# Filler products in the planned idle gaps of TensorE, in an attention and gated-MLP kernel on one core

## The chip, the core and the metric

The kernel runs on one NeuronCore of a Trainium2 chip. Its engines work side by side, each on its own queue in order: TensorE (PE, matrix products into the accumulation memory PSUM), VectorE (DVE), ScalarE (ACT), GpSimd (POOL) and SyncE (SP), which issues the transfers (DMA). The metric is the device time of one execution in microseconds (us); the median of three runs is given, and less is better.

## The reference

Four batches of 8 heads with 768 positions and 64 features go through attention with a causal window of 128 and 4 sink positions, and the result through a gated MLP whose gate mixes positions:

```python
scores = np.where(keep, scale * q @ k.T, -1e9)   # keep: 4 sinks, or 0 <= rel < 128
a = softmax(scores); x = a @ v                   # heads side by side: (4, 768, 512)
h = relu(x @ w_in)                               # 512 -> 1024
u, v = h[..., :512], h[..., 512:]
v_n = (v - mean(v)) / sqrt(var(v) + 1e-6)
v_s = einsum('ts,bsd->btd', w_spatial, v_n) + b_spatial[None, :, None]
out = (u * v_s) @ w_out
```

## The kernel before

The work is cut into tiles of 128 positions, 6 to a batch. For each tile and each half of the heads there is one score product (`sc`, four banks of PSUM), masks and row maxima on DVE (`mask`, line 808), exponentials on ACT, a split of the weights into a high and a low 16-bit part on DVE, ACT or POOL (lines 557 to 573), their transposition by DMA (`pT`), the product with the values (`av`, lines 864 to 876, many small products of 65 columns) and the division by the row sums on DVE (`divide`, lines 878 to 884: `den` and then `x`). After each tile follow the MLP's products `ps_v` and `ps_u`, and per batch `ps_s` and `ps_o`; operands are split in two 16-bit parts, so each product is a sum of three (`three`, line 588). Batch 0's tiles also share the engines with the decoding and splitting of the weights (`w_in`, `w_spatial`, `w_out`), whose scales come from a maximum over all partitions (`all_max`, lines 600 to 624: a row transpose `ps_row` and a column product `ps_col` on PE with reductions on DVE between).

The order of everything is fixed when the kernel is built. Each piece is handed to a `Plan` with a rank (its step plus the entry of its kind in the table `WHEN`), the engines that may run it and an estimated time; `Plan.order` (line 293) then simulates the engines piece by piece with these times, taking the piece that can start earliest, and the pieces are recorded in order of their simulated starts. Each engine runs its part of that order strictly in turn. A ring of buffers is a number of slots; a piece that needs a new buffer has to wait in the plan until one is free.

The `av` ring has two slots, taken from a pool of PSUM banks, one tile to a bank:

```python
BANKS = {"sc": 4, "av": 2, "mm": 2}
IN_TURN = ("u", "vn", "q", "pexp", "pT", "p16", "xT", "x16", "av", "sc", "vraw")
"sc": ("sc", bank("sc")), "av": ("av", bank("av")),
```

The framework puts in the semaphore waits that the recorded order needs: for a tile's readers on its writers, and for a buffer's next writer on its last readers.

Of the kernel before, what the change touches and what calls it, by code (L numbers as in the profile page):

```python
# [6 lines left out]
F32 = mybir.dt.float32  # L7
F32R = mybir.dt.float32r
F16 = mybir.dt.float16
# [10 lines left out]
P = 128  # L20
# [244 lines left out]
GAP = {"o": 0.201, "s": 0.751, "u": 1.654, "v sum": 1.920, "w_in 0": 0.416, "w_in 1": 0.266, "w_out": 1.377, "w_sp": 0.683}  # L265
TOGETHER = 4
IN_TURN = ("u", "vn", "q", "pexp", "pT", "p16", "xT", "x16", "av", "sc", "vraw")
LATENCY = {"PE": 0.25, "d": 0.15, "a": 0.18, "p": 0.12}


# [7 lines left out]


QUEUED = 3.0  # L280


class Plan:

    def __init__(self, rings, ring_of):
        self.pieces, self.rings, self.ring_of = [], rings, ring_of

    def add(self, name, step, b, engines, time, f, reads=(), writes=(), dma=None, shared=False):

# [3 lines left out]
    def order(self):  # L293
# [21 lines left out]
        for i in range(n):  # L315
            for key in ps[i][5] + ps[i][6]:
                base = key[:2]
                ring = self.ring_of.get(base[0])
# [3 lines left out]
        held = {r: [] for r in self.rings}  # L322
        slots = {r: [None] * n for r, n in self.rings.items()}
# [4 lines left out]
        ready = [0.0] * n  # L328
        free = {"PE": 0.0, "d": 0.0, "a": 0.0, "p": 0.0, "SP": 0.0, "port": 0.0}
        moved = 0.0  # L330
        open_ = [i for i in range(n) if not missing[i]]
        out = []

        def room(i):

            t, new = 0.0, {}
            for key in ps[i][5] + ps[i][6]:
                base = key[:2]
                ring = takes.get(base)
                if ring is None or base in taken:  # L340
                    continue
                k = len(held[ring]) + new.get(ring, 0)
                if ring in IN_TURN and turn[ring][k] != base:
                    return None
                j = new[ring] = new.get(ring, 0) + 1
                if ring == "p16":
                    old = slots[ring][k % len(slots[ring])]
                    if old and left[old]:
                        return None
                    t = max(t, until[old] if old else 0.0)  # L350
                    continue
                ends = sorted(until[b] if b else 0.0 for b in slots[ring] if b is None or not left[b])
                if len(ends) < j:
                    return None
                t = max(t, ends[j - 1])
            return t

        while open_:
            best = None
            for i in open_:  # L360
                t = room(i)
                if t is None:
                    continue
                t = max(t, ready[i])
                if ps[i][7] and not ps[i][5]:
                    t = max(t, moved - QUEUED)
                es = ps[i][2] if ps[i][2] not in free else (ps[i][2],)
                cs = []
                for e in es:
                    port = e == "p" or (e == "d" and ps[i][8])  # L370
                    b = max(t, free[e])
                    d = ps[i][3][e] if isinstance(ps[i][3], dict) else ps[i][3]
                    cs.append((max(b, free["port"] if port else 0.0) + d, b, e))
                for c in ((min(cs),) if len(cs) > 1 else cs):
                    c = (c[1], i, c[2])
                    if best is None or c < best:
                        best = c
            if best is None:
                raise RuntimeError("plan: no piece can go on: " + str([(ps[i][0], ps[i][5], ps[i][6]) for i in open_[:16]])
                                   + str({r: [(b, b and left[b]) for b in h] for r, h in slots.items()}))  # L380
            t, i, e = best
            _, _, _, time, f, reads, writes, dma, shared = ps[i]
            d = time[e] if isinstance(time, dict) else time
            if e == "p" or (e == "d" and shared):
                d += max(free["port"] - t, 0.0)
                free["port"] = t + d
            free[e] = t + d
            if dma is None:
                end = t + d + LATENCY[e]
            else:  # L390
                moved = max(t + d + 0.3, moved) + dma
                end = moved + 1.5
            for key in reads + writes:
                base = key[:2]
                ring = takes.get(base)
                if ring and base not in taken:
                    taken.add(base)
                    held[ring].append(base)
                    k = ((len(held[ring]) - 1) % len(slots[ring]) if ring == "p16" else
                         min((until[b] if b else 0.0, k) for k, b in enumerate(slots[ring]) if b is None or not left[b])[1])  # L400
                    for j in users[base]:
                        ready[j] = max(ready[j], until[slots[ring][k]] if slots[ring][k] else 0.0)
                    slots[ring][k] = base
            for base in {k[:2] for k in reads + writes}:
                left[base] -= 1
                until[base] = max(until[base], end)
            open_.remove(i)
            for j in after[i]:
                missing[j] -= 1
                ready[j] = max(ready[j], end)  # L410
                if not missing[j]:
                    open_.append(j)
            out.append((t, len(out), f, e))
        if len(out) != n:
            raise RuntimeError("plan: pieces left")
        self.end = max(until.values())
        return [(f, e) for _, _, f, e in sorted(out, key=lambda x: x[:2])]


# [50 lines left out]
def fast_path(tc, st, qk, v, vs, w_in, w_sp, b_sp, w_out, out):  # L470

    nc = tc.nc
    TC = 256
    VNS = 2.0 ** 10
    with (
# [21 lines left out]
        def sb(shape, dt, tag):  # L497
            return lambda name: work.tile(shape, dt, tag=tag, name=name, bufs=RINGS[tag])

        def bank(tag):  # L500
            return lambda name: ps_all.tile([P, 512], F32, tag=tag, name=name, bufs=BANKS[tag])

        turns = {"p16": 0}

        def next_p16(name):
            turns["p16"] += 1
# [16 lines left out]
            "xT": ("xT", sb([P, 2, KC, TC], F16, "xT")),  # L523
            "g": ("g", sb([P, TC], F32, "g")),
            "g2": ("g2", sb([P, 2, TC], F32R, "g2")),
            "sc": ("sc", bank("sc")), "av": ("av", bank("av")),
            "ps_v": ("mm", bank("mm")), "ps_u": ("mm", bank("mm")), "ps_s": ("mm", bank("mm")),
            "ps_o": ("mm", bank("mm")), "ps_row": ("mm", bank("mm")), "ps_col": ("mm", bank("mm")),
        }
        rings = dict(RINGS, ksink=1, **BANKS)  # L530
        rings.update({f"{kind}{j}": 1 for kind in ("kslot", "vslot", "vsink") for j in range(4)})
        plan = Plan(rings, dict({k: r for k, (r, _) in makers.items()}, **{r: r for r in rings}))
        tiles = {}

        def tl(kind, i):
# [562 lines left out]
```

## Time and profile before

| | us |
|---|---|
| median of 3 runs | 440.31 (439.42 to 442.29) |
| profiled execution | 440.37 |
| its span, first to last instruction | 438.5 |
| TensorE busy in it | 400.7 |
| VectorE busy | 330.2 |
| ScalarE busy | 252.8 |
| GpSimd busy | 129.7 |

The profile is one execution. Busy time is the time in which an engine executes an instruction; weight loads of TensorE (PEld) overlap its products and are counted apart. [...] In the rows in order of time, equal instructions that follow each other are merged, with their count; the bracket at the end is idle time just before, and what ended it. A product's time contains its draining, which overlaps the next product, so the pace is read from the starts.

### The profile page before, as it was taken

How to read it: one execution, taken by the hardware profiler on the slowest of the kernel's cores; microseconds unless marked ns; L12 is line 12 of the kernel's file. 1: busy time of each engine (PE TensorE's matmuls, PEld its weight loads, DVE VectorE, ACT ScalarE, POOL GpSimd, SP SyncE). 2: the span in 40 equal slices, each digit the busy share in tenths (PEclk: the TensorE clock that was granted, in tenths of full speed). 3: DMA queues.
4: the chain of work that ended last, by engine and by line, in shares of the span. 5: the costliest groups of instructions: out<-in, count | busy, mean ns of one | idle time of the engine just before them, and what ended most of it. 6: DMA issues, size and time to landing. Idle time of an engine off the chain costs nothing.

```text
span 438.5 us, 9688 instructions
## 1 busy us (share of the span) xinstructions
PE 400.7 (91%) x3509; PEld 301.9 (69%) x3509; DVE 330.2 (75%) x1048; ACT 252.8 (58%) x561; POOL 129.7 (30%) x192
## 2 busy tenths in 40 slices
PE   1537897899899999999999999999999999999995
PEld 1324454675687777677777768868867788878883
DVE  2899999899988999999898998887470752426350
ACT  3989876897974776688778878843232111010101
POOL 4545623635652314134443166600020200000000
PEclk9999988999999999999999999999999999999998
DMA  6999999899894399999999877946204000010102
GB/s 211 280 350 289 223 212 244 189 226 172 199 241 87 78 211 199 227 200 181 212 220 213 165 177 129 157 90 150 50 25 111 11 1 33 16 72 25 49 24 80
DMA packets 149640, 66.14 MB, mean 151 GB/s; under 512 B 124880, under 2 KB 137936, under 8 KB 149584
## 3 DMA queue, kind: packets, MB, share of 16 engines
q1 hardware_dynamic: 149440, 65.44, 66.3%
q8 instruction: 29, 0.48, 0.5%
q14 instruction: 27, 0.22, 0.2%
q10 hardware_dynamic: 144, 0.00, 0.0%
HBM read 28.72 MB, written 6.29 MB: 80 GB/s over the span
## 4 chain that ended last, share of the span: by engine, by line
PE 75%; DVE 13%; DMA 5%; ACT 2%; issue 2%; SPq 1%; ACTq 0%; DVEq 0%
PE ps_s L591 22%; PE ps_o L591 16%; PE ps_u L591 12%; PE ps_v L591 11%; PE sc L803 8%; DVE pexp L808 3%; PE av L873 2%; PE av L874 2%; PE av L875 2%; DMA q<-qk_t 1%; DMA dec<-w_in 1%; DMA vraw<-v_s 1%; DMA dec<-w_out 1%; DVE p L573 1%; DVE vring L580 1%
## 5 line engine op out<-in xcount | busy, mean ns | idle before, releaser
L591 PE MATMUL ps_s<-wsp,vn 128*128 128x256 f16 x864 | 99.3, 273 | 0.0
L591 PEld LDWEIGHTS <-vn 128*128 128x128 f16 x864 | 83.5, 98 | 12.1 <-issue 2.4
L813 ACT ACTIVATE pexp<-pexp,nm 128x260 f32<-128x260 f32 (+1 forms) x192 | 82.7, 484 | 11.1 <-DVE nm L808 10.5
L803 PE MATMUL sc<-kring,q 64*128 64x260 f32 (+1 forms) x384 | 65.6, 427 | 13.8 <-DMA q<-qk_t 9.2
L591 PE MATMUL ps_u<-xT,win 128*128 128x256 f16 x576 | 69.6, 273 | 2.7 <-ACT vr L916 1.8
L591 PE MATMUL ps_o<-wout,g 128*128 128x512 f32 x288 | 71.0, 400 | 0.0
L591 PE MATMUL ps_v<-win,xT 128*128 128x512 f16 x288 | 68.4, 391 | 0.8 <-DVE allmax_r L619 0.5
L591 PEld LDWEIGHTS <-win 128*128 128x128 f16 x576 | 54.4, 98 | 13.9 <-issue 7.4
L591 PEld LDWEIGHTS ps_o<-wout,g 128*128 128x128 f32 x288 | 53.0, 188 | 13.3 <-issue 0.7
L803 PEld LDWEIGHTS sc<-kring,q 64*128 64x128 f32 x384 | 39.8, 204 | 28.5 <-DVE nm L808 9.2
L573 POOL TENSOR_TENSOR p<-pexp,p 128x16 f16<-128x16 f32 (+2 forms) x43 | 41.9, 981 | 43.7 <-ACT p L557 36.4
L977 DVE SCALAR_TENSOR_TENSOR g<-ps_s,isc,b_bc 128x256 f32<-128x256 f32 x48 | 23.2, 483 | 41.2 <-PE ps_s L591 40.9
L1004 ACT COPY ob<-ps_o 128x512 f32<-128x512 f32 x24 | 14.0, 585 | 66.9 <-PE ps_o L591 66.0
L591 PEld LDWEIGHTS <-xT 128*128 128x128 f16 x288 | 28.2, 100 | 34.2 <-issue 6.3
L956 ACT ACTIVATE u<-ps_u,icu 128x256 f32<-128x256 f32 x48 | 22.7, 472 | 40.4 <-PE ps_u L591 39.8
L873 PE MATMUL av<-vring,pT 128*128 128x65 f16 x352 | 38.7, 197 | 0.9 <-ACT vring L559 0.9
L874 PE MATMUL av<-vring,pT 128*128 128x65 f16 x352 | 38.4, 197 | 0.6 <-DVE vring L580 0.6
L875 PE MATMUL av<-vring,pT 128*128 128x65 f16 x352 | 38.4, 197 | 0.0
L557 ACT CAST p<-pexp 128x32 f16<-128x32 f32 (+2 forms) x65 | 37.6, 599 | 0.8 <-DMA pT<-p 0.5
L573 DVE TENSOR_TENSOR p<-pexp,p 128x1024 f16<-128x1024 f32 (+2 forms) x37 | 36.3, 989 | 0.3 <-ACT p L557 0.3
L873 PEld LDWEIGHTS <-pT 128*128 128x128 f16 x352 | 33.4, 100 | 3.2 <-issue 2.4
L874 PEld LDWEIGHTS <-pT 128*128 128x128 f16 x352 | 33.3, 100 | 1.8 <-issue 0.8
(120 smaller groups left out, 581.6 us busy)
## 6 DMA issues: line engine op xcount, KB each, us to landing
kring<-qk_t SPq DMA_DIRECT2D x24, 256.0 KB, 4.1
q<-qk_t SPq DMA_DIRECT2D x24, 256.0 KB, 4.1
vraw<-v_s SPq DMA_DIRECT2D x24, 256.0 KB, 3.8
out<-ob SPq DMA_DIRECT2D x24, 256.0 KB, 2.0
dec<-w_in SPq DMA_DIRECT2D x8, 512.0 KB, 7.1
wsp<-w_sp_t SPq DMA_DIRECT2D x6, 384.0 KB, 6.5
dec<-w_out SPq DMA_DIRECT2D x4, 512.0 KB, 4.7
pT<-p SPq DMA_TRANSPOSE x96, 3.5
```

The costliest lines, as they stand in the source:

```text
L557: nc.scalar.copy(o, x)
L573: eng[e].tensor_tensor(out=o, in0=x, in1=hi, op=ALU.subtract)
L591: nc.tensor.matmul(o, a, m, start=(i == 0), stop=(i == n - 1))
L803: nc.tensor.matmul(view(h + q)[0], tl("q", (b, t))[rows, hp, :], keys, start=True, stop=True)
L808: nc.vector.tensor_tensor_reduce(out=po, in0=o, in1=mask, scale=-0.125, scalar=3.0e38, op0=ALU.add, op1=ALU.min, accum_out=nm()[:, q:q + 1])
L813: nc.scalar.activation(po, po, AF.Exp, bias=nm()[:, q:q + 1], scale=-1.0)
L873: nc.tensor.matmul(o[:, h], ph, vh, start=(t < 2 and j == 0), stop=False)
L874: nc.tensor.matmul(o[:, h], ph, vl, start=False, stop=False)
L875: nc.tensor.matmul(o[:, h], pl, vh, start=False, stop=(j == nb - 1 and (t < 2 or h == HH - 1)))
L956: plan.add("u relu", r, b, "a", 0.365, lambda e: nc.scalar.activation(tl("u", (b, c0))[:, d, :], tl("ps_u", i)[:, :TC], AF.Relu, scale=val ...
L977: nc.vector.scalar_tensor_tensor(out=g(), in0=tl("ps_s", i)[:, :TC], scalar=vals["s", "sp"][1], in1=b_bc[:, t0:t0 + TC], op0=ALU.mult, op1 ...
L1004: plan.add("o copy", r, b, "a", 0.485, lambda e: nc.scalar.copy(tl("ob", i), tl("ps_o", i)), [("ps_o", i)], [("ob", i)])
```

## The change

After the plan is made, its order is kept, and every idle gap that the plan's own simulation shows on TensorE from 4 us on is looked up. Into each goes a number of filler products that by 0.108 us each would take half of the gap. A filler loads a 16-bit view of the identity matrix as weights and streams 248 columns of the same matrix into columns 264 to 511 of the first value bank; the value products use columns 0 to 259, so nothing reads the fillers' result. To have a fixed place for them, the two value banks become one tile `avs` with two halves that are used alternately (`next_av`), and `STRICT` makes the plan alternate too.

```diff
--- before.py
+++ after.py
@@ -265,6 +265,7 @@
 GAP = {"o": 0.201, "s": 0.751, "u": 1.654, "v sum": 1.920, "w_in 0": 0.416, "w_in 1": 0.266, "w_out": 1.377, "w_sp": 0.683}
 TOGETHER = 4
 IN_TURN = ("u", "vn", "q", "pexp", "pT", "p16", "xT", "x16", "av", "sc", "vraw")
+STRICT = ("p16", "av")
 LATENCY = {"PE": 0.25, "d": 0.15, "a": 0.18, "p": 0.12}
 
 
@@ -278,12 +279,13 @@
 
 
 QUEUED = 3.0
+WARM_FROM, WARM_SHARE, WARM_ONE = 4.0, 0.5, 0.108
 
 
 class Plan:
 
-    def __init__(self, rings, ring_of):
-        self.pieces, self.rings, self.ring_of = [], rings, ring_of
+    def __init__(self, rings, ring_of, warm):
+        self.pieces, self.rings, self.ring_of, self.warm = [], rings, ring_of, warm
 
     def add(self, name, step, b, engines, time, f, reads=(), writes=(), dma=None, shared=False):
 
@@ -328,6 +330,7 @@
         ready = [0.0] * n
         free = {"PE": 0.0, "d": 0.0, "a": 0.0, "p": 0.0, "SP": 0.0, "port": 0.0}
         moved = 0.0
+        busy = [(0.0, WARM_FROM)]
         open_ = [i for i in range(n) if not missing[i]]
         out = []
 
@@ -343,7 +346,7 @@
                 if ring in IN_TURN and turn[ring][k] != base:
                     return None
                 j = new[ring] = new.get(ring, 0) + 1
-                if ring == "p16":
+                if ring in STRICT:
                     old = slots[ring][k % len(slots[ring])]
                     if old and left[old]:
                         return None
@@ -385,6 +388,8 @@
                 d += max(free["port"] - t, 0.0)
                 free["port"] = t + d
             free[e] = t + d
+            if e == "PE":
+                busy.append((t, t + d))
             if dma is None:
                 end = t + d + LATENCY[e]
             else:
@@ -396,7 +401,7 @@
                 if ring and base not in taken:
                     taken.add(base)
                     held[ring].append(base)
-                    k = ((len(held[ring]) - 1) % len(slots[ring]) if ring == "p16" else
+                    k = ((len(held[ring]) - 1) % len(slots[ring]) if ring in STRICT else
                          min((until[b] if b else 0.0, k) for k, b in enumerate(slots[ring]) if b is None or not left[b])[1])
                     for j in users[base]:
                         ready[j] = max(ready[j], until[slots[ring][k]] if slots[ring][k] else 0.0)
@@ -414,6 +419,10 @@
         if len(out) != n:
             raise RuntimeError("plan: pieces left")
         self.end = max(until.values())
+        for (_, t), (t1, _) in zip(busy, busy[1:]):
+            count = int((t1 - t) * WARM_SHARE / WARM_ONE)
+            if count:
+                out.append((t + 0.05, len(out), self.warm(count), "PE"))
         return [(f, e) for _, _, f, e in sorted(out, key=lambda x: x[:2])]
 
 
@@ -500,7 +509,20 @@
         def bank(tag):
             return lambda name: ps_all.tile([P, 512], F32, tag=tag, name=name, bufs=BANKS[tag])
 
-        turns = {"p16": 0}
+        avs = ps_all.tile([P, 2, 512], F32, tag="avs", name="avs", bufs=1)
+        turns = {"p16": 0, "av": 0}
+
+        def next_av(name):
+            turns["av"] += 1
+            return avs[:, (turns["av"] - 1) % 2]
+
+        def warm(count):
+            lead, follow = st.ident.bitcast(F16)[:, :P], st.ident.bitcast(F16)[:, :248]
+
+            def f(e):
+                for _ in range(count):
+                    nc.tensor.matmul(avs[:, 0, 264:], lead, follow, start=True, stop=True)
+            return f
 
         def next_p16(name):
             turns["p16"] += 1
@@ -523,13 +545,13 @@
             "xT": ("xT", sb([P, 2, KC, TC], F16, "xT")),
             "g": ("g", sb([P, TC], F32, "g")),
             "g2": ("g2", sb([P, 2, TC], F32R, "g2")),
-            "sc": ("sc", bank("sc")), "av": ("av", bank("av")),
+            "sc": ("sc", bank("sc")), "av": ("av", next_av),
             "ps_v": ("mm", bank("mm")), "ps_u": ("mm", bank("mm")), "ps_s": ("mm", bank("mm")),
             "ps_o": ("mm", bank("mm")), "ps_row": ("mm", bank("mm")), "ps_col": ("mm", bank("mm")),
         }
         rings = dict(RINGS, ksink=1, **BANKS)
         rings.update({f"{kind}{j}": 1 for kind in ("kslot", "vslot", "vsink") for j in range(4)})
-        plan = Plan(rings, dict({k: r for k, (r, _) in makers.items()}, **{r: r for r in rings}))
+        plan = Plan(rings, dict({k: r for k, (r, _) in makers.items()}, **{r: r for r in rings}), warm)
         tiles = {}
 
         def tl(kind, i):
```

The plan itself comes out as before: with the fillers left out, every engine has the same instructions in the same order, and the general path behind the branch at the end isn't run. 210 fillers are added, each a weight load and a product. Their groups, in order: 5, 6, 5, 9, 13, 3, 19, 20, 6, 9, 22, 6, 2, 10, 9, 12, 9, 5, 1, 17, 4, 2, 1, 3, 1, 5, all before 100 us of the plan, and 6 near its end.

In the built program the waits are set by tile. Six divides (their first instruction, `den`) wait for a count of PE's semaphore that is reached only with the last filler of the group recorded ahead of them: behind the first two value products (22 fillers), the third (10), the fourth (12), the fifth (9), the sixth (1) and the fourteenth (5). Five fillers wait for a divide. Where a divide is recorded ahead of the next value product, that product now waits for it, though it writes the other half.

On TensorE at the beginning (`sc` is the score product of one tile and half of the heads; a count at the end merges equal rows), before:

```order
L803 MATMUL sc<-kring,q 128x128 x8
L803 MATMUL sc<-kring,q 128x260 x8
L608 MATMUL ps_row<-ident,allmax_m 1x128
L615 MATMUL ps_col<-allmax_304,ones 128x1
L608 MATMUL ps_row<-ident,allmax_m 1x128
```

and now:

```order
L524 LDWEIGHTS ident
L524 MATMUL avs<-ident 128x248
L825 MATMUL sc<-kring,q 128x128 x4
L524 LDWEIGHTS ident
L524 MATMUL avs<-ident 128x248
```

The first two score products stood next to each other; now 5 fillers stand ahead of the first and 6 between the two.

On TensorE behind the first two value products (`av`, then `avs`; the last row before is the next score product), before:

```order
L873 LDWEIGHTS pT
L873 MATMUL av<-vring,pT 128x65
L874 LDWEIGHTS pT
L874 MATMUL av<-vring,pT 128x65
L875 LDWEIGHTS pT
L875 MATMUL av<-vring,pT 128x65
L803 MATMUL sc<-kring,q 128x260 x4
```

and now:

```order
L896 LDWEIGHTS pT
L896 MATMUL avs<-vring,pT 128x65
L897 LDWEIGHTS pT
L897 MATMUL avs<-vring,pT 128x65
L524 LDWEIGHTS ident
L524 MATMUL avs<-ident 128x248
```

22 fillers stand between the last of the value products and the score product.

On VectorE, around the divides of these two products, now (names in brackets are the semaphores that an instruction waits for):

```order
L766 SCALAR_TENSOR_TENSOR vsink_137<-vsraw,v_scale,vsink_137 32x4x64 [waits DMAHW4_49]
L673 SCALAR_TENSOR_TENSOR w_467<-dec,w_467 128x512 [waits DMAHW2_49,DVE_49]
L903 TENSOR_SCALAR den<-avs 128x4 [waits PE_49]
L904 RECIPROCAL den<-den 128x4 [waits DVE_49]
L905 TENSOR_TENSOR x<-avs,den 128x256 [waits DVE_49]
L903 TENSOR_SCALAR den<-avs 128x4
```

Nothing moved here. The first `den` waits for the last of the 22 fillers, where it waited for the last of its own products; the second, which had a wait of its own, needs none behind it.

## Rows read from the trace of the kernel before

**Rows 1.** The page's first part: TensorE's busy us, share, instructions.

```profile
PE 400.7 (91%) x3509; PEld 301.9 (69%) x3509; DVE 330.2 (75%) x1048; ACT 252.8 (58%) x561; POOL 129.7 (30%) x192
```

**Rows 2.** Busy time by stretch: busy us by engine, granted clock, DMA share.

```profile
core 0: us, PE busy (x) PEld busy (x) DVE busy (x) ACT busy (x) POOL busy (x), PEclk, DMA share, GB/s
9.00:20.00 11.00, 7.62 (x33) 5.25 (x33) 10.01 (x44) 9.51 (x23) 3.94 (x5) 1.00 1.11 321
20.00:30.00 10.00, 2.36 (x9) 1.87 (x10) 8.75 (x25) 8.03 (x19) 5.19 (x3) 1.00 1.05 301
30.00:41.00 11.00, 7.98 (x38) 4.33 (x36) 10.77 (x35) 11.00 (x24) 5.90 (x7) 1.00 1.11 326
41.00:48.00 7.00, 6.70 (x40) 3.62 (x41) 6.62 (x20) 4.49 (x13) 6.01 (x6) 1.00 0.94 181
53.00:59.00 6.00, 5.55 (x41) 3.99 (x41) 5.25 (x21) 5.55 (x16) 3.29 (x3) 0.72 1.05 258
120.00:430.00 310.00, 310.00 (x2790) 242.14 (x2787) 224.30 (x699) 155.69 (x345) 72.31 (x101) 1.00 0.56 120
```

**Rows 3.** Waits of VectorE, first 125 us: total us, times, longest.

```profile
DVE den L881 <- PE av L875: 2.2, 3, 0.8
```

**Rows 4.** Order of time, TensorE: start, length, engine, line, work, idle before.

```profile
34.92 0.25 PE L874 MATMUL av<-vring,pT 128*128 128x65 f16 x1
34.98 0.24 PE L875 MATMUL av<-vring,pT 128*128 128x65 f16 x1
51.22 0.19 PE L874 MATMUL av<-vring,pT 128*128 128x65 f16 x1
51.25 0.20 PE L875 MATMUL av<-vring,pT 128*128 128x65 f16 x1
96.61 1.47 PE L591 MATMUL ps_u<-xT,win 128*128 128x256 f16 x12
```

**Rows 5.** Order of time: first two value products, and their divide.

```profile
33.79 0.22 PE L874 MATMUL av<-vring,pT 128*128 128x65 f16 x1 [0.64 <-DVE vring L580]
34.89 0.15 DVE L881 TENSOR_SCALAR den<-av 128x4 f32<-128x4 f32 x1
```

**Rows 6.** Order of time: third value product and divide.

```profile
41.30 0.37 PE L608 MATMUL ps_row<-ident,allmax_m 128*1 128x128 f32 x1 [0.72 <-DVE allmax_m L605]
42.92 0.58 PE L615 MATMUL ps_col<-allmax,ones 1*128 1x1 f32 x2
43.15 0.14 DVE L881 TENSOR_SCALAR den<-av 128x4 f32<-128x4 f32 x1
```

**Rows 7.** Order of time: around the fourth and fifth value product.

```profile
51.76 0.15 DVE L881 TENSOR_SCALAR den<-av 128x4 f32<-128x4 f32 x1
52.50 0.42 DVE L808 CUSTOM_DVE_ANT_0 pexp<-sc,m_odd 128x260 f32<-128x260 f32 x1
52.84 0.42 DVE L808 CUSTOM_DVE_ANT_0 pexp<-sc,m_odd 128x260 f32<-128x260 f32 x1
52.98 2.28 PE L803 MATMUL sc<-kring,q 64*128 64x260 f32 x8 [1.54 <-DVE nm L808]
56.95 0.16 DVE L881 TENSOR_SCALAR den<-av 128x4 f32<-128x4 f32 x1 [0.68 <-PE av L875]
```

**Rows 8.** Order of time, TensorE and VectorE, the start.

```profile
8.99 2.70 PE L803 MATMUL sc<-kring,q 64*128 64x128 f32 x16 [8.99 <-DMA q<-qk_t]
11.37 0.28 DVE L808 CUSTOM_DVE_ANT_0 pexp<-sc,m_first 128x128 f32<-128x128 f32 x1
29.28 0.69 DVE L641 TENSOR_SCALAR_CACHE_REDUCE w<-w 128x512 f32<-128x512 f32 x1 [0.74 <-ACT w L645]
```

**Rows 9.** Order of time: TensorE's last wait; a product behind a divide.

```profile
111.07 1.47 PE L591 MATMUL ps_u<-xT,win 128*128 128x256 f16 x12 [1.81 <-ACT vr L916]
190.12 0.43 DVE L883 TENSOR_TENSOR x<-av,den 128x256 f32<-128x256 f32 x1
190.46 0.19 PE L873 MATMUL av<-vring,pT 128*128 128x65 f16 x1
```

## The prediction

> **What bounds the kernel now.** I read the page's totals first, then busy time by stretch, then the waits, then the order of time around the places that change. TensorE (PE) is busy 400.7 us, 91% of the span [rows 1], so it looks like the bound everywhere. By stretch it is not [rows 2]. From 120 to 430 us PE is busy all 310.00 us: that part is PE's. Before it PE has room (2.36 of 10 us from 20 to 30) and VectorE (DVE) has none: 10.01 of 11, 8.75 of 10, 10.77 of 11 and 6.62 of 7 us in the four stretches from 9 to 48. PE's last wait of any size is the 1.81 us before 111.07 [rows 9], for an activation that stands behind DVE's work. So the end is the moment at which PE resumes there, plus some 327 us of PE work without a gap. A change before 111 us counts only by what it does to DVE's chain; a PE instruction added after 111 us counts in full.
>
> PE also runs slowly early. The granted clock is printed as 1.00 before 47 us, but the records tell otherwise: at 34.92 and 34.98 us products of 65 columns start 55 ns apart, at 51.22 and 51.25 us 30 ns [rows 4]. [...] Later the clock falls again: 0.72 over 53 to 59 us [rows 2], which includes scores (2.28 us) that follow 1.54 us of idling [rows 7]. All this slowness has cost DVE little: up to 125 us it waited for a value product 2.2 us, three times [rows 3].
>
> **The change, part by part.** 210 fillers (each a weight load and a product of 248 columns) go into 27 places on PE: 26 groups before 100 us of the plan, one of six near the end. No other engine's instructions and no transfer change places, so SP's, ScalarE's and GpSimd's queues are as before. Two things come with it: fillers stand in PE's queue ahead of real products, and they write the tile that the divides read.
>
> Price of one filler: twelve products of 256 columns take 1.47 us, the last 0.27 of it draining [rows 4], so (1.47 - 0.27) / 11 = 0.109 us each, 0.105 for 248 columns. At the low level I scale the 55 ns of 65 columns: 0.21. Which of the two holds is the open question; I price each place by both.
>
> *Place A, 22 fillers behind the first two value products.* In the built program the first divide's wait on PE's semaphore is met only by the last of these fillers, not by the product itself. Before, the products run from 33.79 and DVE comes to the divide at 34.89 without waiting [rows 5]. After, 23 further products at 0.030 end the issue at 34.5, 22 fillers add 2.3, completion 0.25: 37.1. DVE stands still 2.2 us. At the low level: the products' issue ends at 35.0, 4.6 more, completion: 39.9, a stall of 5.0. Everything of DVE's queues behind that divide, and ScalarE waits for it for masks and for x.
>
> *Place B, 2 and 10 fillers around the third value product.* The row transpose waits for DVE, at 41.30 [rows 6], and keeps its distance to it. From there: 0.21 for two fillers, 0.72 for 24 products, 1.05 for ten fillers, 0.15 to complete, and 0.65 for the transpose and the column product, which took 0.37 and 0.58 on the slow clock: 44.1. DVE wants the divide at 43.15 [rows 6]: 0.95 us. At the low level 3.1.
>
> *Place C, 12 fillers behind the fourth.* Products start their last at 51.25 [rows 4]; plus 0.03, 1.26 and 0.15 gives 52.7 against the divide at 51.76 [rows 7]: 0.9 us. At the low level 2.9.
>
> *Place D, 9 fillers behind the fifth.* Here the clock pays. Before, scores ran 2.28 us and the divide at 56.95 waited 0.68 [rows 7]. At the high level the scores go at the pace of DVE's masks, which start 0.34 us apart (52.50, 52.84 [rows 7]), and end near 54.3, the products at 55.3, fillers at 56.4; DVE, without its wait, arrives at 56.95 - 0.68 = 56.27. The wait falls from 0.68 to 0.13: a gain of 0.55. At the low level a loss of 1.9.
>
> *The start.* The first two score groups run back to back, 16 passes in 2.70 us from 8.99, and DVE takes the second's first mask at 11.37 [rows 8]. Six fillers between them, at the low level, are 1.26 us, and DVE loses at most that. Groups of 5, 9 and 13 follow, perhaps still at the low level (5.7 us). DVE later waits 0.74 for ScalarE's half of a decoded weight [rows 8], a wait that starts with a load and so takes a part back. I take 0.5, nearer to the 1.26 less 0.74, with bounds 0 and 3.
>
> *Elsewhere before 111 us.* The groups of 6, 3, 19, 20, 6, 9, 6, 9, 5, 1, 17 and the seven small ones stand where the next product waits for DVE or a transfer anyway, or where DVE comes later than they end; cover: those waits (1.54 us [rows 7], 1.81 us [rows 9]). I take 0; a group at the low level may outgrow its cover, which is in the range.
>
> *One tile for two.* Both value banks are now one tile, and a product recorded behind the previous divide waits for it, though it is in the other bank. Where PE is the bound I compared each product's start with the divide before it: one is too early, 190.46 against 190.12 + 0.43 [rows 9]. 0.2 us, bounds 0 and 0.5.
>
> *The six near the end.* No wait there: 6 x 0.105 = 0.6 us, in full.
>
> Sum at the high level: 2.2 + 0.95 + 0.9 - 0.55 + 0.5 + 0.2 + 0.6 = 4.8 us. The profiled execution took 440.37 (span 438.5 and 1.9 around it), 0.06 over the median of 440.31. Forecast: **445.2 us**, 1.1% slower. At the low level throughout: 5.0 + 3.1 + 2.9 + 1.9 + 3 + 0.5 + 0.6 = 17, or 457.
>
> [...]
>
> [...]
>
> **Rivals.**
>
> *DVE's stalls are swallowed (not slower).* In the stretches from 9 to 48 us the DMA share is 0.94 to 1.11 [rows 2], as full as DVE; were a transfer due behind each stall that comes no earlier anyway, A, B and C would cost nothing, and the six late fillers and the shared tile leave 441.2 us. It decides at the first DVE wait for a transfer behind 35 us: the stalls must be followed by one at least 4 us long. Against it: the only such wait is the 0.74 at 29.28 [rows 8], ahead of place A; behind it DVE is full. For it: ScalarE, which feeds DVE, does wait for loads. Chance 0.2, and most of it gives back only a part.
>
> *The fillers do not keep the clock.* Then they cost double and the stalls grow; all low 457, half of the extra 12 us 451. For: the falls after 1.54 us. Against: A begins behind real products, and 22 fillers in a row are themselves dense work. Chance 0.17.
>
> *The clock's gain reaches the end.* [...] From rows: PE's 24.7 busy us from 9 to 48 [rows 2] could shrink by 12, which would give 429 if PE bounded that stretch. But DVE idles only 2.9 us of those 39, so at most that comes back: 438.1, within 1%. Chance 0.05.
>
> **How the numbers follow.** The forecast's own case has 0.58, the rivals 0.2, 0.17 and 0.05. The forecast's own range is 442.5 to 449 (a few places off by half a microsecond, or one or two of them low). For 8 in 10 I go from 441.0 (stalls swallowed) to 451.0 (half of the places low). About 1%, 4.4 us, can be told from no change. The forecast case lies across that line at 444.7: two thirds of it beyond, so slower 0.58 x 0.67 + 0.17 = 0.56; faster 0.03, out of the third rival and what I may have missed of the first; same 0.41.
>
> **What would show it.** Right: DVE's divide rows after the first two, third and fourth value products wait 2.2, 0.95 and 0.9 us, released by PE's filler; PE's last wait lies near 115 us in place of 111; behind it the same work and 0.6 us more; 65-column products before 47 us start 30 ns apart. Wrong: divides without idle time before them, or DVE idle after 35 us with a transfer as its releaser; fillers at 0.21 us apiece at places A to D; the resumption of PE at or before 111 us.

## The result, and the profile after the change

The changed kernel takes **445.22 us** (median of 6 runs, 444.61 to 448.18) against 440.19 us (6 runs): a ratio of 1.0128, 95% interval 1.0088 to 1.0169. The forecast was 445.2. The profiled execution is the shortest of the six, 444.61 us; its span is 442.8, 4.3 more than before. The page's first part answers to [rows 1]:

```profile
PE 413.8 (93%) x3719; PEld 315.1 (71%) x3719; DVE 329.4 (74%) x1048; ACT 253.2 (57%) x561; POOL 129.6 (29%) x192
```

PE is busy 13.1 us more, DVE's work is the same. By stretch, to set against [rows 2] (length, then busy us and instructions of PE, PEld, DVE, ACT, POOL, then TensorE's granted clock as a share of full speed, DMA share, GB/s):

```profile
9.00:20.00 11.00, 9.43 (x69) 6.71 (x69) 9.77 (x43) 9.50 (x23) 3.89 (x5) 1.00 1.11 319
20.00:30.00 10.00, 6.31 (x54) 5.03 (x54) 8.54 (x23) 7.91 (x19) 5.20 (x3) 1.00 1.03 318
30.00:41.00 11.00, 7.43 (x68) 5.11 (x66) 8.71 (x31) 8.82 (x17) 4.27 (x5) 1.00 1.11 304
41.00:48.00 7.00, 6.45 (x51) 4.61 (x52) 5.12 (x12) 4.64 (x11) 5.28 (x6) 0.76 0.93 187
53.00:59.00 6.00, 4.42 (x47) 3.29 (x46) 5.02 (x18) 4.42 (x10) 2.25 (x2) 1.00 0.92 273
120.00:430.00 310.00, 310.00 (x2792) 240.99 (x2790) 227.31 (x711) 158.37 (x351) 73.70 (x102) 1.00 0.58 122
```

PE still has no gap from 120 to 430 us. DVE, full before, now idles 2.3 of 11 us from 30 to 41 and 1.9 of 7 from 41 to 48. What it waits for, to set against [rows 3] (us in all, times, longest):

```profile
DVE den L903 <- PE avs L524: 5.2, 4, 2.1
...
DVE den L903 <- PE avs L897: 0.7, 1, 0.7
```

L524 is the filler's line, L903 the divide's. The places A, B, C and D in order of time, the fillers on PE (at B also two of the value products) and the divides on DVE, to set against [rows 5, 6, 7]:

```profile
35.08 2.49 PE L524 MATMUL avs<-ident 128*128 128x248 f16 x22
...
37.60 0.16 DVE L903 TENSOR_SCALAR den<-avs 128x4 f32<-128x4 f32 x1 [2.05 <-PE avs L524]
...
44.19 0.62 PE L524 MATMUL avs<-ident 128*128 128x248 f16 x2
...
45.12 0.24 PE L895 MATMUL avs<-vring,pT 128*128 128x65 f16 x1
45.17 0.24 PE L896 MATMUL avs<-vring,pT 128*128 128x65 f16 x1
...
46.54 1.23 PE L524 MATMUL avs<-ident 128*128 128x248 f16 x10
...
47.81 0.16 DVE L903 TENSOR_SCALAR den<-avs 128x4 f32<-128x4 f32 x1 [1.86 <-PE avs L524]
...
54.87 1.43 PE L524 MATMUL avs<-ident 128*128 128x248 f16 x12
...
56.34 0.16 DVE L903 TENSOR_SCALAR den<-avs 128x4 f32<-128x4 f32 x1 [0.91 <-PE avs L524]
...
60.10 1.11 PE L524 MATMUL avs<-ident 128*128 128x248 f16 x9
...
61.25 0.16 DVE L903 TENSOR_SCALAR den<-avs 128x4 f32<-128x4 f32 x1 [0.39 <-PE avs L524]
```

Four divides stand still with the filler as releaser: 2.05, 1.86, 0.91 and 0.39 us. PE's last wait of any size, and the first mask of the second score group, to set against [rows 9] and [rows 8]:

```profile
114.36 1.47 PE L613 MATMUL ps_u<-xT,win 128*128 128x256 f16 x12 [1.28 <-ACT vr L938]
...
12.31 0.29 DVE L830 CUSTOM_DVE_ANT_0 pexp<-sc,m_first 128x128 f32<-128x128 f32 x1 [0.88 <-PE sc L825]
```

PE resumes at 114.36 in place of 111.07, 3.29 us later. The loss until then is on DVE's queue, whose 1048 instructions stand in the same order in both kernels, so their lag can be read instruction by instruction (the table under "Why").

### The profile page after: what moved, and what is told of

It reads as the page before. It is cut to its first block, busy times and chain, and to the rows that moved or that the text cites. A ratio compares the mean times of both kernels' runs of the same rounds, so it can differ in the third digit from the quotient of the medians.

```text
span 442.8 us, 10100 instructions
## 1 busy us (share of the span) xinstructions
PE 413.8 (93%) x3719; PEld 315.1 (71%) x3719; DVE 329.4 (74%) x1048; ACT 253.2 (57%) x561; POOL 129.6 (29%) x192
## 4 chain that ended last, share of the span: by engine, by line
PE 79%; DVE 13%; DMA 3%; issue 2%; SPq 1%; ACT 1%; ACTq 0%; DVEq 0%
PE ps_s L613 21%; PE ps_o L613 15%; PE ps_u L613 12%; PE ps_v L613 11%; PE sc L825 9%; DVE pexp L830 3%; PE avs L895 2%; PE avs L896 2%; PE avs L524 2%; PE avs L897 2%; DMA q<-qk_t 1%; DMA dec<-w_in 1%; DVE x L905 1%; DVE wsp L602 1%; DVE vring L602 1%
## 5 line engine op out<-in xcount | busy, mean ns | idle before, releaser
L613 PE MATMUL ps_v<-win,xT 128*128 128x512 f16 x288 | 65.6, 379 | 1.1 <-ACT vr L938 0.8
L825 PE MATMUL sc<-kring,q 64*128 64x260 f32 (+1 forms) x384 | 58.7, 396 | 8.3 <-DVE nm L830 5.2
L595 POOL TENSOR_TENSOR p<-pexp,p 128x16 f16<-128x16 f32 (+2 forms) x43 | 40.9, 957 | 44.5 <-ACT p L579 27.8
L825 PEld LDWEIGHTS sc<-kring,q 64*128 64x128 f32 x384 | 35.6, 191 | 22.9 <-DVE nm L830 8.7
L896 PE MATMUL avs<-vring,pT 128*128 128x65 f16 x352 | 37.3, 194 | 0.7 <-DVE vring L602 0.7
L895 PE MATMUL avs<-vring,pT 128*128 128x65 f16 x352 | 37.5, 195 | 0.4 <-ACT vring L581 0.4
L897 PE MATMUL avs<-vring,pT 128*128 128x65 f16 x352 | 37.3, 194 | 0.0
L895 PEld LDWEIGHTS <-pT 128*128 128x128 f16 x352 | 32.8, 98 | 2.8 <-issue 1.7
L524 PE MATMUL avs<-ident 128*128 128x248 f16 x210 | 28.5, 280 | 6.1 <-POOL m_second L465 4.7
```

The source lines that it names most:

```text
L524: nc.tensor.matmul(avs[:, 0, 264:], lead, follow, start=True, stop=True)
L595: eng[e].tensor_tensor(out=o, in0=x, in1=hi, op=ALU.subtract)
L613: nc.tensor.matmul(o, a, m, start=(i == 0), stop=(i == n - 1))
L825: nc.tensor.matmul(view(h + q)[0], tl("q", (b, t))[rows, hp, :], keys, start=True, stop=True)
L895: nc.tensor.matmul(o[:, h], ph, vh, start=(t < 2 and j == 0), stop=False)
L896: nc.tensor.matmul(o[:, h], ph, vl, start=False, stop=False)
```

## The experiments

The theory on trial: a divide waits for the fillers recorded ahead of it *because they write the tile that it reads*; DVE's queue stands behind it, and this lag reaches the end. Rivals: the fillers cost by their place in PE's queue, ahead of real products ("queue"); the two value banks as one tile cost ("shared tile"); each stall is hidden by a transfer ("swallowed"). Each run edits the changed kernel in the loop that places the groups; groups are numbered from 0 in the order listed with the change, so 10, 13, 15 and 16 are A's 22, B's 10, C's 12 and D's 9 fillers, and 26 is the late six. The lines that only number the groups are left out of the edits shown; three dots stand for lines not shown. A ratio is against the kernel before, in the same session, with its 95% interval.

### 1. No fillers, one tile for the two banks

```diff
             count = int((t1 - t) * WARM_SHARE / WARM_ONE)
+            count = 0
```

> All 210 fillers left out; the two value banks stay one tile. Theory (divides wait for the fillers recorded ahead of them, since fillers and values share a tile): 440.3 us, within 0.4 of the kernel before; the divide's waits on TensorE stay near 2.2 us. Rival 'shared tile' (ordering value products behind the previous divide is what costs): 443 to 445. Rival 'queue' (fillers cost because they stand ahead of real products on TensorE): 440.3 too.

Measured: 440.61 us, before 440.63; 1.0008 (0.998 to 1.0037). The times show no cost of the shared tile, but the interval, -0.9 to 1.6 us, is too wide for the 0.2 us of the forecast; the rows show 0.14 (under "Why"). That is not the loss.

### 2. All fillers where they stand, four groups into another tile

The number of the group has moved on by one where it is tested, hence `group - 1`:

```diff
-                out.append((t + 0.05, len(out), self.warm(count), "PE"))
+                count = count
+                group += 1
+            if count:
+                out.append((t + 0.05, len(out), self.warm(count, group - 1 in {10, 13, 15, 16}), "PE"))
...
-        def warm(count):
+        def warm(count, apart=False):
...
+                own = bank("mm")("own") if apart else avs[:, 0]
                 for _ in range(count):
-                    nc.tensor.matmul(avs[:, 0, 264:], lead, follow, start=True, stop=True)
+                    nc.tensor.matmul(own[:, 264:], lead, follow, start=True, stop=True)
```

> All 210 fillers in their places; only the groups of 22, 10, 12 and 9 behind the first five value products write a tile of the 'mm' banks, the others the value tile as in the change. Theory: the divides behind these products wait for their own products alone (0.7 us at most, in place of 2.05, 1.86, 0.91 and 0.39), though as many fillers stand ahead of as many products on TensorE; what is left is the start, the six late ones and a share for the clock: 440.3 to 441.8. Rival 'queue' (the place on TensorE costs, not the tile): 444.5 to 448.

Measured: **440.98 us**, before 441.04; 1.0007 (0.9978 to 1.0037). The same 210 fillers stand in the same 27 places of PE's queue (read from the traces of both); the first five divides on DVE:

```profile
36.06 0.16 DVE L908 TENSOR_SCALAR den<-avs 128x4 f32<-128x4 f32 x1 [0.41 <-PE avs L902]
...
36.81 0.15 DVE L908 TENSOR_SCALAR den<-avs 128x4 f32<-128x4 f32 x1
...
44.34 0.14 DVE L908 TENSOR_SCALAR den<-avs 128x4 f32<-128x4 f32 x1
...
52.84 0.15 DVE L908 TENSOR_SCALAR den<-avs 128x4 f32<-128x4 f32 x1
...
57.26 0.15 DVE L908 TENSOR_SCALAR den<-avs 128x4 f32<-128x4 f32 x1
```

The waits of 2.05, 1.86, 0.91 and 0.39 us are gone but for 0.41, which is released by a value product (L902) and no filler. This separates the tile from the place: "queue" and "shared tile" fall as explanations, and nearly the whole loss goes with the tile that the four groups write.

An earlier try had put *every* group into a tile of these banks:

```diff
+                own = bank("mm")("own")
                 for _ in range(count):
-                    nc.tensor.matmul(avs[:, 0, 264:], lead, follow, start=True, stop=True)
+                    nc.tensor.matmul(own[:, 264:], lead, follow, start=True, stop=True)
```

> The same 210 fillers in the same places, but each group writes a fresh tile of the two 'mm' banks, which no divide reads. Theory: the divides behind the first value products wait no more for fillers (2.05, 1.86 and 0.91 us of waits gone), start +0.6, late six +0.7, the later clock gain -1 stays: 439.8 to 441. Rival 'queue': the fillers are as many and stand where they stood: 444 to 445.5. Rival 'shared tile' (value banks still one tile): 444 to 445.

Measured: 448.01 us; 1.0185 (1.0139 to 1.0231), far off what the theory gave. In order of time, the 17 fillers of group 19 on PE, and the divide behind the next value product on DVE:

```profile
72.53 3.67 PE L529 MATMUL own<-ident 128*128 128x248 f16 x17 [4.98 <-ACT vr L943]
...
77.65 0.16 DVE L908 TENSOR_SCALAR den<-avs 128x4 f32<-128x4 f32 x1 [4.77 <-PE avs L902]
```

Up to 67 us no divide waits for a filler there either. Then group 19 needs a bank of which ScalarE has not yet read the last content (`vr`): the fillers wait 4.98 us, the products queue behind them, the divide waits 4.77. Fillers in a ring that is in use are a new wait; the first five products come at a time when that ring is free.

### 3. Six groups left out, then five

Without the groups behind which a divide waits (10, 13, 15, 16, 18 and 25):

```diff
+                count = 0 if group in {10, 13, 15, 16, 18, 25} else count
```

> Only the six groups that a divide waits for are left out (22, 10, 12, 9, 1 and 5 fillers); 151 stay. Theory: 440 to 441, no divide waits for a filler; the clock may fall again near 53 to 59 us, worth up to 0.6. Rival 'queue', by share of fillers: 440.2 + 5 x 151/210 = 443.8. Rival 'shared tile': 444 to 445.

Measured: 443.17 us; 1.0055 (1.0031 to 1.0078), 2 to 3 us over the theory's figure. Not one divide waits for a filler. Two stretches by busy time, and the products of 512 columns in the second:

```profile
104.00:108.00 4.00, 2.08 (x22) 1.44 (x22) 3.94 (x8) 4.00 (x10) 1.55 (x1) 1.00 0.97 198
108.00:112.00 4.00, 4.00 (x12) 1.45 (x13) 3.79 (x19) 1.79 (x4) 2.24 (x4) 0.57 1.16 222
...
107.92 4.45 PE L617 MATMUL ps_v<-win,xT 128*128 128x512 f16 x12 [1.03 <-ACT vring L585]
```

PE is busy 2.08 of 4 us from 104 to 108; then the clock is 0.57, and twelve products that take 2.75 us in the changed kernel, at a clock of 1.00, take 4.45. This is where PE becomes the bound: over these rows and the gap ahead of them PE's lag behind the kernel before grows from 0.48 to 2.45 us. Put back the five fillers of group 25, which stand just there (the edit against the last one):

```diff
-                count = 0 if group in {10, 13, 15, 16, 18, 25} else count
+                count = 0 if group in {10, 13, 15, 16, 18} else count
```

> As the run without the six groups (443.2), but the five fillers behind the fourteenth value product, at 108.5 us, are put back. That run's clock was 0.57 of full from 108 to 112 us, and twelve 512-column products took 4.45 in place of 2.75 us. Theory: the five fillers keep the clock there; 1.7 us come back: 441 to 442. Rival (what is left costs by count or by queue): 443.2 or a little more.

Measured: 441.78 us; 1.0035 (1.0016 to 1.0054). The same two views:

```profile
108.00:112.00 4.00, 3.34 (x23) 1.99 (x22) 3.79 (x17) 2.89 (x7) 2.03 (x3) 1.00 0.69 158
...
107.25 2.76 PE L617 MATMUL ps_v<-win,xT 128*128 128x512 f16 x12 [0.45 <-DMA xT<-x]
```

The clock stays at 1.00, the twelve products take 2.76 us, and PE's lag stays where it was (0.93, then 0.91 us). By the medians five fillers, half a microsecond of PE, bring back 1.4 us; the two intervals overlap, so the 1.7 us by which the twelve products grew are the firmer number. The divide that has to wait for these five comes later than they end.

### 4. The 22 fillers alone, none of them, twice as many

The 22 alone:

```diff
+                count = count if group == 10 else 0
```

> Only the 22 fillers behind the first two value products. [...] Time 441 to 444. Rival 'queue': the scores behind them are delayed, the divide does not wait; rival 'swallowed': 440.3.

Measured: 444.01 us; 1.0075 (1.0034 to 1.0116). The fillers on PE and the divide on DVE:

```profile
35.18 4.62 PE L528 MATMUL avs<-ident 128*128 128x248 f16 x22
...
39.84 0.16 DVE L907 TENSOR_SCALAR den<-avs 128x4 f32<-128x4 f32 x1 [4.72 <-PE avs L528]
```

The 22 start 0.206 us apart, where the forecast put 0.21 for the low level, and the divide waits 4.72 us, 5.0 in the forecast's low case. In the changed kernel's trace, with the groups ahead of them, they had cost 0.106; those groups do not make it certain, for in experiment 2's trace, with the same ones ahead, the 22 start 0.141 apart on average. DVE is 4.95 us behind the kernel before at this divide and still 3.57 at the tenth, so "swallowed" falls. The profiled execution, 446.17 us, is one of the slower of its eight: after a gap of 2.14 us on PE the twelve products of experiment 3 took 4.45 us here too, and 2.0 us more were lost. By the medians the 22 cost 3.4 us, near the 3.57 that are left without this second loss.

All but the 22:

```diff
+                count = 0 if group == 10 else count
```

> All fillers but the 22 behind the first two value products. Theory (the stall at the 22 makes TensorE idle 1.98 us ahead of the scores, this lowers the clock, and so the ten fillers behind the third product cost double): not only the 2.05 us wait goes, the third product's divide waits 0.95 instead of 1.86 us, and 65-column products there start 30 instead of 55 ns apart. Time 441.5 to 443. Rival 'each group by itself': 445.2 - 2.1 = 443, and the third product's divide still waits 1.9 us at 55 ns a product.

Measured: 444.5 us; 1.0101 (1.0055 to 1.0147): 0.7 less than with them by the medians, within both intervals, where 2.1 or more was expected by either theory. By stretch, and the divide behind the fifth product:

```profile
30.00:41.00 11.00, 9.08 (x49) 5.46 (x48) 10.03 (x34) 10.35 (x20) 4.81 (x6) 0.54 1.12 295
41.00:48.00 7.00, 7.00 (x56) 4.80 (x56) 5.90 (x16) 3.97 (x11) 5.55 (x6) 0.76 1.06 214
...
61.56 0.16 DVE L907 TENSOR_SCALAR den<-avs 128x4 f32<-128x4 f32 x1 [1.96 <-PE avs L528]
```

My reason for the low clock at B (PE idle ahead of the scores, behind the stall) falls: without the 22 and their stall the clock is low there all the same, and already from 30 us (0.54). The third divide waits 0.65 (ten fillers that start 0.107 apart), as hoped, but D's nine run at 0.204 us and the fifth divide waits 1.96 in place of 0.39. Taking one stall away shifted what followed into other clock states; part of the price is paid elsewhere.

And 44 of them:

```diff
+                count = 2 * count if group == 10 else count
```

> The 22 fillers behind the first two value products doubled to 44, all else as changed. Theory: the divide waits 22 x 0.110 = 2.4 us longer there (4.4 to 4.5), and the end is 1.5 to 2.5 us later than in the changed kernel: 446.7 to 447.7 (if the one falls into a slot that a transfer sets anyway, less). Rival 'swallowed': 445.2. Rival 'queue by count': 5.0 x 22/210 = 0.5 us more.

Measured: 449.69 us; 1.0207 (1.0153 to 1.0262), 4.5 over the changed kernel. The divide:

```profile
42.72 0.16 DVE L907 TENSOR_SCALAR den<-avs 128x4 f32<-128x4 f32 x1 [5.42 <-PE avs L528]
```

It waits 5.42 us, 3.37 more. Of it 2.3 are the 22 added (0.106 apiece); the rest is the low clock that the value products and the first four fillers met in this execution. DVE came to this divide 1.75 us later than in the changed kernel already; the span is 5.3 us longer. So the 3.4 us of the longer wait reach the end in full.

### 5. Sixty late fillers

```diff
+                count = 10 * count if group == 26 else 0
```

> Only the late group, ten times as many: 60 fillers near the end, where TensorE never waits, and none elsewhere. Theory: each costs its issue, 60 x 0.105 to 0.110 = 6.3 to 6.6 us in full: 446.7 to 447.1. Rival (late fillers are covered by something): 440.5.

Measured: 446.47 us, before 440.3; 1.0148 (1.0108 to 1.0188), that is 6.2 us. In the trace the 60 start 0.106 us apart, and PE is 6.4 us later behind them than ahead of them. Here a PE instruction behind 115 us is paid in full.

### 6. The first ten groups alone

These are 95 fillers, up to 33 us, and no divide waits for them. In the changed kernel, which has them too, the two runs of eight scores of 260 columns from 13.14 and 15.28 us take 1.15 and 1.25 us, where before they took 2.17 and 2.44 (from 11.85 and 14.63).

```diff
+                count = count if group < 10 else 0
```

> [...] Theory: VectorE sets the pace there, so the clock buys nothing and the 0.94 us wait behind the second score group comes back within 3 us; 440 to 441. Rival 'the clock's gain reaches the end': 438.1. Rival 'start costs 3': 443.

Measured: 442.79 us; 1.0041 (1.0016 to 1.0065), above what I expected. In order of time, a value product on PE, and two later divides on DVE:

```profile
72.15 0.29 PE L893 MATMUL avs<-vsink,pT 96*128 96x260 f16 x1 [4.08 <-DMA pT<-p]
...
79.46 0.16 DVE L907 TENSOR_SCALAR den<-avs 128x4 f32<-128x4 f32 x1 [1.31 <-PE avs L901]
...
84.76 0.16 DVE L907 TENSOR_SCALAR den<-avs 128x4 f32<-128x4 f32 x1 [0.84 <-PE avs L901]
```

DVE is 1.3 us behind the kernel before at the first divide (36.17 against 34.89), 0.8 of it from the start and 0.42 from that divide's own wait for value products. As much again comes at 72 us, where none of these fillers stands: PE waits 4.08 us for a transposition (before: 2.26), so that the value product starts 2.84 us later than before (72.15 against 69.31), and the divide behind it waits 1.31 us. The clock falls in this stretch in both kernels (0.89 from 67 to 74 us, 0.78 before), so it does not explain the difference. Why the transposition came later here stays open. That the clock's gain before 33 us reaches the end is refuted.

### 7. Only the groups that pay

Groups from 60 to 110 us alone, then with those from 50 us on, C's and D's into the `mm` tile as in experiment 2:

```diff
+                count = count if group in {17, 19, 20, 21, 22, 23, 24, 25} else 0
```

> Only the eight groups from 60 to 110 us but the single filler behind the sixth product: 38 fillers, none at the late place. [...] Rival (a filler costs wherever it stands, 0.02 us apiece): 441.2.

Measured: 441.32 us, where I had expected 439.2 to 440.3, with the clock high at 71 us, the tenth divide's wait of 0.83 us gone and nothing paid; 1.0005 (0.9982 to 1.0028): no loss, no gain that can be told, though in the trace the clock is 1.00 from 67 to 74 us (0.78 before) and the tenth divide waits no more.

```diff
+                count = count if group in {14, 15, 16, 17, 19, 20, 21, 22, 23, 24, 25} else 0
```

> The groups from 50 to 110 us; those behind the fourth and fifth value product (12 and 9) write a tile of the 'mm' banks, which no divide reads; none before and none late. Theory: as the run with the later groups alone, and the fall of the clock from 54 to 57 us goes too, whose wait was 0.68: 438.7 to 440.0, at most 0.3% faster than the kernel before. Rival (the clock's gains do not reach the end): 440.3.

Measured: **439.92 us**, before 441.04; 0.9976 (0.9955 to 0.9997). The stretch that had 0.72 before [rows 2], and two divides that waited 0.68 [rows 7] and 0.83 us:

```profile
53.00:59.00 6.00, 5.58 (x54) 3.76 (x52) 5.93 (x24) 5.85 (x16) 3.71 (x3) 1.00 1.13 257
...
56.72 0.16 DVE L908 TENSOR_SCALAR den<-avs 128x4 f32<-128x4 f32 x1
...
81.30 0.16 DVE L908 TENSOR_SCALAR den<-avs 128x4 f32<-128x4 f32 x1
```

The clock is 1.00 there and neither divide waits. Over the whole span the granted clock is 0.996 to 0.999 in eleven of the twelve runs and 0.968 in one; in the kernel before it is 0.995 at most. This is the best of the placements tried: some 1 us, a quarter of a percent (0.1 to 2.0 us by the interval).

## Why the prediction held, and where its steps did not

The table has DVE's lag (PE's in the rows that name it): the start of an instruction in the changed kernel less its start before, and what each step added, beside the forecast's term.

| step | before | after | lag | added | forecast |
|---|---|---|---|---|---|
| first mask of the second score group | 11.37 | 12.31 | 0.94 | | |
| reduction of `w` (the start) | 29.28 | 29.84 | 0.56 | 0.56 | 0.5 |
| first divide (A) | 34.89 | 37.60 | 2.71 | 2.15 | 2.2 |
| third divide (B) | 43.15 | 47.81 | 4.66 | 1.95 | 0.95 |
| `win_scale` | 46.59 | 49.95 | 3.36 | -1.30 | 0 |
| `icu` | 47.48 | 51.20 | 3.72 | 0.36 | 0 |
| fourth divide (C) | 51.76 | 56.34 | 4.58 | 0.86 | 0.9 |
| fifth divide (D) | 56.95 | 61.25 | 4.30 | -0.28 | -0.55 |
| tenth divide | 82.30 | 85.61 | 3.31 | -0.99 | 0 |
| PE resumes | 111.07 | 114.36 | 3.29 | -0.02 | 0 |
| PE's product of [rows 9] (one tile) | 190.46 | 193.88 | 3.42 | 0.13 | 0.2 |
| PE's last product (late six) | 432.62 | 436.71 | 4.09 | 0.67 | 0.6 |
| span | 438.5 | 442.8 | 4.3 | 0.2 | 0 |

**The bound** was right: PE full from 120 to 430 us, the loss collected on DVE before PE resumes.

**The filler's price** was right at both levels: 0.106 us apart at the high one (forecast 0.105), 0.206 at the low one (0.21). That the places would be met at the high one was my estimate; no run shows what sets the level, and the same 22 start 0.106, 0.141 and 0.206 us apart in three traces. **A and C** are right within 0.05 us; that A met the high level is this execution's state, for elsewhere the same 22 cost 4.72 us (experiment 4).

**B** was mis-sized twice, and the two errors nearly cancel. The clock was 0.76 from 41 to 48 us; the products there start 55 ns apart (45.12, 45.17 us), where I had named 30 ns as a sign, the two fillers ahead of them 0.206 us, and the wait is 1.86 us, between my bounds of 0.95 and 3.1. Then 1.30 us come back at an instruction that I had not looked at. Before, in order of time on DVE and on GpSimd (POOL); and in the changed kernel:

```profile
44.92 1.63 DVE L222 SCALAR_TENSOR_TENSOR win_exp<-win_not,win_exp 128x1 int32<-128x1 int32 x1
...
44.32 2.22 POOL L573 TENSOR_TENSOR p<-pexp,p 128x16 f16<-128x16 f32 x2
```

```profile
49.60 0.32 DVE L222 SCALAR_TENSOR_TENSOR win_exp<-win_not,win_exp 128x1 int32<-128x1 int32 x1
...
49.23 0.68 POOL L595 TENSOR_TENSOR x<-x,x 128x256 f16<-128x256 f32 x1
```

Both times the operation on 128x1 elements ends as a pass of POOL's does: 46.55 and 46.54 before, 49.92 and 49.91 after. Before, it began 1.63 us ahead of that end; after, DVE came to it with only 0.32 us of a pass left. In all 14 kept traces it ends within 0.02 us behind the end of a pass of POOL's, after 0.32, 0.41 or 1.63 us. That fits a wait for POOL; no run took POOL's pass away to show it. A lag is not only passed on: it also changes whom the later work meets.

**D** gave 0.28 in place of 0.55. The clock was high, as forecast, but the eight scores took 1.75 us from 57.57, ending some 0.4 later behind the fourth divide than I had put them, so the fillers still held the divide for 0.39 us.

**"Elsewhere: 0"** failed, to the good. The seventeen fillers at 71.44 us stand in the gap of PE behind which the clock had fallen before. Before (the first row is that stretch by busy time) and after, in order of time, products of 512 columns on PE and the tenth divide on DVE:

```profile
67.00:74.00 7.00, 4.45 (x40) 2.55 (x39) 6.90 (x21) 5.20 (x15) 1.05 (x2) 0.78 0.93 224
...
72.27 3.75 PE L591 MATMUL ps_v<-win,xT 128*128 128x512 f16 x12 [0.29 <-ACT vr L916]
...
82.30 0.16 DVE L881 TENSOR_SCALAR den<-av 128x4 f32<-128x4 f32 x1 [0.83 <-PE av L875]
```

```profile
76.57 2.75 PE L613 MATMUL ps_v<-win,xT 128*128 128x512 f16 x12 [0.76 <-ACT vr L938]
...
85.61 0.16 DVE L903 TENSOR_SCALAR den<-avs 128x4 f32<-128x4 f32 x1
```

The clock of that stretch was 0.78 before, and is 1.00 after. Twelve products take 2.75 in place of 3.75 us, and the 0.83 us wait is gone. I had named the fall at 53 us and let this one pass under "cover", though [rows 3] counts three waits of DVE and I had used one. That it was the seventeen that kept the clock is not shown by this trace alone: in the traces of experiment 1 (no fillers) and of the 22 alone, with DVE 3.8 and 4.6 us behind, the clock is 1.00 there too, the twelve products take 2.75 us and the tenth divide doesn't wait. A later DVE met another clock; in the last run of experiment 7, with these fillers, it is 1.00 there with DVE within 0.1 us of the kernel before.

**The start** agrees in size (0.56 for 0.5) and not in its steps, which is luck. Of the 0.94 us lost all but 0.15 is back within 3 us. The rest arises at 29.28 us [rows 8], in DVE's wait for ScalarE's half of a decoded weight: I had this wait take a part back, and it grew from 0.74 to 1.15 us. In the five kept traces without a filler ahead of that instruction (experiments 1 and 5, the 22 alone, and both of experiment 7) it starts between 0.85 us earlier and 2.22 later than before, so a row of one trace can't tell a cost of the fillers there.

**One tile** was right in kind and place, 0.13 us for 0.2. In the changed kernel the product named in [rows 9] starts only behind the end of the divide, 0.48 us after the start of its last operation, where it had been 0.34:

```profile
193.40 0.42 DVE L905 TENSOR_TENSOR x<-avs,den 128x256 f32<-128x256 f32 x1
...
193.88 0.19 PE L895 MATMUL avs<-vring,pT 128*128 128x65 f16 x1
```

PE's lag grows there by 0.13 to 0.15 us in every kept trace with the one tile, the one without fillers too. **The late six** are 0.81 us with their draining, 0.67 on PE's end; 0.2 more in the span, behind PE's last product, have no row that explains them.

So the sum, 4.8 against 4.3 of span, was met by its main terms and by luck in the rest: +1.0 at B and +0.4 behind it stand against -1.3 and -1.0 that I had not seen, and the start's 0.5 was met by another cause. The rival "swallowed" (chance 0.2) is refuted by the runs with 22, 44 and the other tile: no transfer hid the stall. "The fillers do not keep the clock" is refuted for most places, but its price is real: the run with the 22 alone shows the low case to within 0.3 us. "The clock's gain reaches the end" was right in kind, wrong in place: nothing that shows before 33 us, 1.3 us from D and the tenth divide together.

What put A, B and C into the sum is the tile, for which the built program sets the wait. The fillers write the first half of `avs`, one bank; the value products take the halves in turn (`next_av`), so the divides of A, B and D read that bank, and the fourth, C's, reads the other. It waited 0.91 us all the same, beside 2.05 and 1.86 us at A and B. With fillers in another tile the waits are gone (experiment 2); two tiles of one bank each, as before, with fillers in one of them, weren't run. What the chip does with a filler and a divide in one bank at a time is not shown: no run has such an access without a wait.

Open: two of the six runs of the changed kernel took 448.1 us, at a granted clock over the whole span of 0.980 and 0.981, where the other four had 0.988 to 0.996. In five of the experiments the nine fillers at 32 to 35 us ran at 0.204 us apiece, in the profiled run of the change at 0.107; a start of A on the low clock would give such a step, but no trace of a 448 us run shows it.

## What to carry to other kernels

A product that nothing reads is not free if it writes a tile that someone else reads: the reader waits for it, here even the one that reads the tile's other half (0.91 us at C), and everything behind the reader on its engine waits too. Before filling idle time of an engine, look who sets the pace in that stretch; the fillers pay only where the slowed engine's own late result is what the bound engine waits for, which here was two waits of 0.68 and 0.83 us, and there they have to write a tile that no waiting reader shares and that is free at that time. A sum of stalls is good to about 1 us in a kernel whose engines meet each other: check what each delayed instruction will find beside it.

## What the runs showed of the hardware that was not expected

A gap on PE just ahead of its dense part can cost twice: in the run without six groups 2.08 busy of 4 us were followed by 4 us at a granted clock of 0.57, and twelve products took 1.7 us longer where PE becomes the bound; in the run with the 22 alone the same came behind a gap of 2.14 us. The length of one gap does not settle it: the kernel before idles 1.81 us ahead of 111.07 [rows 9], and its clock is 1.00 in the 4 us from 111 on.

A part of the kernel's spread (438.5 to 444.3 us in one session) can begin with a transfer, with no filler in the program. In the profiled run of experiment 1, at 443.61 us, ScalarE waited for the weights (us in all, times, longest, between 20 and 34 us; before, then that run):

```profile
ACT wtmp L643 <- DMA dec<-w_in: 1.2, 2, 0.9
```

```profile
ACT wtmp L669 <- DMA dec<-w_in: 3.8, 2, 3.1
```

That is 2.6 us more; DVE is 2.2 us behind the kernel before at 29 us, and 2.8 when PE resumes. Differences of that size between two single traces prove nothing in this kernel unless the row with the wait is shown.
